# Tying each two-input GpSimd step to a VectorE step in a fused attention and gated-FFN kernel

## The chip, the cores and the metric

The kernel runs on one core of one Trainium2 chip. The metric is the device time of one execution in microseconds (us); lower is better. TensorE runs at one of two clock levels, 2.4 GHz (granted clock 1.00 in the profile) or 1.2 GHz (0.50).

## The reference

The reference first does attention over 8 batches, 8 heads, 576 positions and a head size of 64, with rotary position embedding on q and k, and then a gated feed-forward block:

```
q_rot, k_rot = rotate(q), rotate(k)                       # x1*cos - x2*sin, x1*sin + x2*cos
scores = matmul(q_rot, k_rot^T) / sqrt(64);  attn = softmax(scores)
x = matmul(attn, v)                                       # heads side by side: 576 x 512 a batch
gate_pre = sum over k = 0..4 of conv_w[k] * x shifted by k positions
out = (sigmoid(gate_pre) * (x @ w_val)) @ w_out
```

All of it is in fp32.

## The kernel before, in words

The work is cut into 32 pairs of heads (four pairs are one batch). All 32 pairs are unrolled. For a pair p the steps are:

- q and k are loaded with their halves also swapped, so that the rotation is two multiplications by a table (`rope_mul`, L275) and one addition (`rope_add`, L279). `qk_hi` (ScalarE) rounds the result to TensorE's fp32r type, and `qk_lo` (L303 for q, L306 for k) keeps the remainder; scores are made of three products of such parts.
- `s_mm` (TensorE, L331) makes scores of 128 rows by 576 in PSUM; there are two such score banks. `s_max` (VectorE, L337) reads them from PSUM and finds each row's maximum, `s_exp` (ScalarE, L345) reads them again and writes the exponentials to SBUF. A score bank is free for the next `s_mm` only after its `s_exp`.
- `t_mm` (TensorE) transposes the exponentials into PSUM, `t_copy` (ScalarE L430, VectorE L432) copies them to SBUF, `pv_mm` and `pv_left` (TensorE, L441 and L451) multiply by v. `r_inv` (VectorE, L461) inverts the sums, and `x_norm` (VectorE, L492, one input in PSUM) scales.
- `x_hi` (ScalarE) and `x_lo` (GpSimd, L505) split x as above. `tap` (VectorE, L518, taps 1 to 4) adds up the convolution, two SBUF inputs each, and `gate` (ScalarE) is its activation.
- After each fourth pair comes that batch's feed-forward part: `f_mm` (TensorE, L558) in two stages, `y_mul` (VectorE, L566, one input in PSUM), `y_hi` (ScalarE), `y_lo` (GpSimd, L573) and `o_out`.
- In the first quarter `weight_step` decodes the weights to such parts (L594 to L606, VectorE, ScalarE and GpSimd).

GpSimd's part is therefore 230 steps, each with two SBUF inputs: 63 `rope_mul`, 45 `rope_add`, 10 `qk_lo`, 15 `weight_step`, 33 `x_lo`, 64 `y_lo`.

What order do they run in? The jobs of all pairs are listed first with what each reads and writes. `ORDER`, a table of 3,327 entries, then says in which order they are issued; a letter after a number names the engine where there is a choice (V VectorE, A ScalarE, G GpSimd). Each engine works through its own entries in the order of the table. Between engines, only data holds a step back: a wait on a semaphore is made where a step reads or overwrites what another engine's step makes or uses. So GpSimd may run ahead of VectorE's place in the table, or fall behind it, as far as the data lets it. For instance, this is a piece of the table, where 1636 is `tap` 2 of pair 15 (VectorE), 1782V a `t_copy` and 1643 a `y_mul` on VectorE, and 1961G is one `rope_mul` of pair 19 on GpSimd:

```
1636 1966 1824:01 1782V 1643:0 1961G
```

Nothing ties 1961G to 1636; it waits for its input's DMA and for the buffers.

Of the kernel before, what the change touches and what calls it, by code (L numbers as in the profile page):

```python
# [10 lines left out]
F32 = mybir.dt.float32  # L11
# [3 lines left out]
AF = mybir.ActivationFunctionType  # L15
ALU = mybir.AluOpType
AX = mybir.AxisListType
# [8 lines left out]
G0 = 256  # L26
G1 = 320
SCALE = 0.125
W = 640
RAW = 1  # L30
# [134 lines left out]
"""  # L165
FILLS = {11: (32, 0), 17: (7, 1), 50: (19, 0), 63: (14, 2), 89: (7, 3), 101: (7, 0), 183: (2, 3), 287: (2, 1), 425: (2, 2)}


class Plan:

# [12 lines left out]

        self.jobs.append((engines, fn, args, r.split(), w.split()))

    def run(self, engine, fill):

        writer, sees = {}, []
        for i, (_, _, _, r, w) in enumerate(self.jobs):
            sees.append([writer.get(t) for t in r + w])  # L190
            writer.update(dict.fromkeys(w, i))
        writer = {}
        for step, entry in enumerate(ORDER.split()):
            entry, _, slots = entry.partition(":")
            i = int(entry.rstrip("VAG"))
            engines, fn, args, r, w = self.jobs[i]
            assert [writer.get(t) for t in r + w] == sees[i], entry
            writer.update(dict.fromkeys(w, i))
            if step in FILLS:
                fill(*FILLS[step])  # L200
            self.slots = [int(x) for x in slots]
            fn(*args, *([engine[entry[-1]]] if len(engines) > 1 else []))
            assert not self.slots, entry


@with_exitstack
def attn_gated_ffn(ctx: ExitStack, tc: tile.TileContext, q2, k2, v2, tab, w_val, conv_w, w_out, out, collect=None):
# [11 lines left out]
    NP = q2.shape[0]  # L219
    NB = out.shape[0]  # L220
    PPB = NP // NB
    V, A, G, T, SP = nc.vector, nc.scalar, nc.gpsimd, nc.tensor, nc.sync
# [7 lines left out]
    plan = Plan()  # L230
# [9 lines left out]
    table = const.tile([128, 2, W], F32, name="tab")  # L240
# [10 lines left out]
    xs = [const.tile([128, 4 + S], F32, name=f"x{i}") for i in range(2)]  # L251
    sums = [const.tile([128, 9], F32, name=f"sums{i}") for i in range(2)]

    state = {}
# [17 lines left out]

    def rope_mul(p, n, i, a, b, eng):
        t = ins[n]
        eng.tensor_tensor(out=t[:, i, a:b], in0=t[:, 0 if p < RAW else i, a:b], in1=table[:, i, a:b], op=ALU.mult)  # L275

    def rope_add(p, n, a, b, eng):
        t = ins[n][:, :, a:b]
        eng.tensor_tensor(out=t[:, 0], in0=t[:, 0], in1=t[:, 1], op=ALU.add)  # L279

    def rope_mm(p, n, a, b):

# [5 lines left out]
    def rotated(p, n, a, b):  # L288
        return state[p][f"b{n}{a}"][:, 0:b - a] if p < RAW else ins[n][:, 0, a:b]
# [9 lines left out]
    def qk_lo(p, n, a, b, eng=V):  # L299
        at = D if n == "k" else 0  # L300
        t = state[p][n][:, :, a + at:b + at]
        if n == "q":
            V.scalar_tensor_tensor(out=t[:, 1], in0=rotated(p, n, a, b), scalar=SCALE, in1=t[:, 0].bitcast(F32),  # L303
                                   op0=ALU.mult, op1=ALU.subtract)
        else:
            eng.tensor_tensor(out=t[:, 1], in0=rotated(p, n, a, b), in1=t[:, 0].bitcast(F32), op=ALU.subtract)  # L306

    def k_wrap(p):

# [24 lines left out]
    def s_max(p, i):  # L334
        st = state[p]
        st[f"nm{i}"] = ring("nm", [128, 1], F32, "nm")
        V.tensor_reduce(out=st[f"nm{i}"], in_=st[f"s{i}"], axis=AX.XY, op=ALU.max, negate=True)  # L337

    def s_exp(p, i, t, part):

# [60 lines left out]
    def t_copy(p, key, eng):  # L401
        both = key[:2] == "h1" and p < NP - 1
        bank = state[p]["bm" + key[2] if both else "b" + key]
        if key[0] == "m":
            x = "ab".index(key[1])
            src = bank[:, 0:256].rearrange("p (j x) -> p j x", x=D)
            dst = turned(p, 1)[:, x * 4:x * 4 + 4, 256:320]
        elif both:
            at = 128 + "ab".index(key[2]) * D
            src = bank[:, 256:384].rearrange("p (h x) -> p h x", h=2)  # L410
            dst = turned(p, "r")[:, :, at:at + D]
        elif key == "hm":
            src = bank[0:D, 0:128].rearrange("p (h x) -> p h x", h=2)
            dst = turned(p, "r")[0:D, :, 256:320]
        elif key[0] == "h" and p == NP - 1:
            rows = HEAD[1 - int(key[1])]
            src = bank[rows].rearrange("p (h x) -> p h x", h=2)
            dst = turned(p, "r")[rows, :, 0:256]
        elif key[0] == "h":
            at = int(key[1]) * 128  # L420
            src = bank[:, 0:256].rearrange("p (h x) -> p h x", h=2)
            dst = turned(p, "r")[:, :, at:at + 128]
        else:
            c = int(key[0])
            g = c // 2
            at = (c - 2 * g) * 128 + "ab".index(key[1]) * D
            src = bank.rearrange("p (s x) -> p s x", x=D)
            dst = turned(p, g)[:, :, at:at + D]
        if eng is A:
            A.copy(out=dst, in_=src)  # L430
        else:
            V.tensor_copy(out=dst, in_=src)  # L432

    def pv_mm(p, g, part):
        st = state[p]
# [22 lines left out]
    def r_inv(p, g):  # L458
        for a, b in COLS[g]:
            r = sums[p % 2][:, a:b]  # L460
            V.tensor_scalar(out=r, in0=r, scalar1=1e-9, scalar2=None, op0=ALU.add)  # L461
            V.reciprocal(out=r if p == NP - 1 else state[p]["pm"][:, 1, a:b], in_=r)

    def r_mm(p, g):
        bank = ring("ps_t", [128, 512], F32, "ps_r", psum)
# [23 lines left out]

    def x_norm(p, g):  # L490
        n = G1 if g else G0
        V.tensor_tensor(out=xs[p % 2][:, 4 + g * G0:4 + g * G0 + n], in0=state[p][f"a{g}"][:, 0:n],  # L492
                        in1=state[p]["rb"][:, g * G0:g * G0 + n], op=ALU.mult)

    def x_hi(p, a, b):
# [5 lines left out]
    def x_lo(p, a, b):  # L501
        st = state[p]
        if "xl" not in st:
            st["xl"] = ring("pl", [128, S], F32R, "xl")
        G.tensor_tensor(out=st["xl"][:, a:b], in0=xs[p % 2][:, 4 + a:4 + b], in1=st["xh"][:, a:b].bitcast(F32), op=ALU.subtract)  # L505

    def tap(p, k, a, b):
        st = state[p]
        c = p % PPB
        x_sb = xs[p % 2]  # L510
        w = cw[:, c * TAPS + k:c * TAPS + k + 1]
        if k == 0:
            if "g" not in st:
                st["g"] = ring("pg", [128, S], F32, "g")
            A.activation(out=st["g"][:, a:b], in_=x_sb[:, a:b], func=AF.Copy, scale=w)  # L515
        else:
            g = st["g"][:, a:b]
            V.scalar_tensor_tensor(out=g, in0=x_sb[:, a + k:b + k], scalar=w, in1=g, op0=ALU.mult, op1=ALU.add)  # L518

    def gate(p, a, b):  # L520

# [20 lines left out]
    ffn = {}  # L542
# [17 lines left out]
    def y_mul(b, dc, lo, hi):  # L560
        n = hi - lo
        if b not in ffn:
            ffn[b] = [ring(f"y{x}", [128, NCH, S], F32R, f"y{x}") for x in range(2)]
        y = ring("yy", [128, G1], F32, "y")[:, 0:n]
        ffn[b, "y", dc, lo] = y
        V.scalar_tensor_tensor(out=y, in0=state[b * PPB + dc]["g"][:, lo:hi], scalar=1.0, in1=ffn[b, 0, dc, lo][:, 0:n],  # L566
                               op0=ALU.add, op1=ALU.mult)

    def y_hi(b, dc, lo, hi):
        A.copy(out=ffn[b][0][:, dc, lo:hi], in_=ffn[b, "y", dc, lo])  # L570

    def y_lo(b, dc, lo, hi):
        G.tensor_tensor(out=ffn[b][1][:, dc, lo:hi], in0=ffn[b, "y", dc, lo], in1=ffn[b][0][:, dc, lo:hi].bitcast(F32),  # L573
                        op=ALU.subtract)

    def o_out(b, oc, lo, hi, eng):
        n = hi - lo
        o = ring("oo", [128, G1], F32, "o")[:, 0:n]
        if eng is A:
            A.activation(out=o, in_=ffn[b, 1, oc, lo][:, 0:n], func=AF.Copy, scale=0.5)  # L580
        else:
            V.tensor_scalar(out=o, in0=ffn[b, 1, oc, lo][:, 0:n], scalar1=0.5, scalar2=None, op0=ALU.mult)
        ffn[b, "o", oc, lo] = o

    def o_dma(b, oc, lo, hi):
        SP.dma_start(out=out[b, oc * 128:(oc + 1) * 128, lo:hi], in_=ffn[b, "o", oc, lo])
# [22 lines left out]
    taps = []  # L609
# [5 lines left out]
        taps.extend(decode(st, tmp, whole=cw))  # L615

    def tap_step(i):
        taps[i]()

    wsteps = {}  # L620

# [8 lines left out]
                              w_hi[n][:, c, m:m + x], w_lo[n][:, c, m:m + x])  # L630

    def weight_step(n, i, k, *eng):
        wsteps[n, i][k](*eng)

    def load_tab(a, b):
        A.dma_start(out=table[:, :, a:b], in_=tab[0, :, :, a:b])
# [40 lines left out]
    for p in range(NP):  # L677
# [7 lines left out]
        for n in ("k", "q"):  # L685
            cut = 288 if n == "k" else 384
            for a, b in [(0, wide[n])] if p else [(0, cut), (cut, wide[n])]:
                half = R2 if p else (1,) if a else (0,)
                x0, x1, hi, lo = (toks(f, half) for f in (f"{n}in#0.@", f"{n}in#1.@", f"{n}{par}#hi.@", f"{n}{par}#lo.@"))
                tr = toks("tab@", [i for i, (u, v) in enumerate(((0, 288), (288, S), (S, W))) if a < v and u < b])  # L690
                add("S", load, p, n, a, b, w=x0 if p < RAW else x0 + " " + x1)
                if p < RAW:
                    add("GV", rope_mul, p, n, 1, a, b, r=tr + " " + x0, w=x1)
                    add("GV", rope_mul, p, n, 0, a, b, r=tr, w=x0)
                    for i, (x, y) in enumerate(((0, cut), (cut, wide[n]))):
                        if not a <= x < b:
                            continue
                        bank, hi, lo = f"ps_t/{n}{p}.{i}", f"{n}{par}#hi.{i}", f"{n}{par}#lo.{i}"
# [13 lines left out]
        for i, c in enumerate(order(p) + (4,)):  # L712
            r = kr + f" k{par}#w" * (i % 2) + " " + toks(f"q{par}#@.@", ("hi", "lo"), (0,) if c < 3 else R2)
            add("P", s_mm, p, c, i % 2, r=r, w=toks(f"ps_s/{p}.@", (2 * c, 2 * c + 1)[:1 + (c < 4)]))
            for x in (2 * c, 2 * c + 1)[:1 + (c < 4)]:
                t = f"{i // 2}{x % 2}" if c < 4 else "m"
# [5 lines left out]
        for key in [str(c) for c in order(p)] + ["m", "h0"] + ["h1"] * last + ["hm"]:  # L722
            g = "r" if key[0] == "h" else 1 if key in ("m", "2", "3") else 0
            if key in ("m", "hm"):
                r = f"p/{p}.m#8" + f" p/{p}.m#r" * (key == "hm" and not last)
                if key == "m" and not last:
                    r += " " + " ".join(f"p/{p}.1{h}#{2 * c + h}" for c in order(p)[2:4] for h in R2)
            elif key[0] == "h":
                i = int(key[1])
                r = " ".join(f"p/{p}.{i}{h}#{2 * c + h}" for c in order(p)[2 * i:2 * i + 2] for h in R2)  # L730
# [72 lines left out]
                    add("S", o_dma, b, *a, r=f"oo/{b}.{j}")  # L803
    if collect is not None:
        return plan
    with tc.manual_schedule():
        plan.run({"V": V, "A": A, "G": G}, fill)


# [57 lines left out]
```

## Time and profile before

| | |
|---|---|
| median of 3 runs | 695.62 us (695.5 to 698.72) |
| the profiled execution | 699.4 us, with a span of 697.5 us on the core |
| busy share of the span | TensorE 96%, VectorE 84%, ScalarE 72%, GpSimd 44% |

The profile is one execution, with each instruction's start and duration. An engine's busy share is an average over the whole span, so the stages have to be looked at apart. The chain of work that ended last is followed back from the last instruction: at each step to what released it, or to the instruction in front on its own engine. Matmuls are pipelined, and their ends are modelled.

### The profile page before, as it was taken

Reading aid. Unit: us, or ns where it says so; the run is one execution under the profiler, and the core shown is the slowest. Engines: PE = TensorE matmul, PEld = TensorE weight load, DVE = VectorE, ACT = ScalarE, POOL = GpSimd, SP = SyncE. Lnnn points to the kernel's source line nnn. Section 1 sums busy time; section 2 is a strip of 40 time slices with the busy share of each in tenths; the row PEclk is TensorE's granted clock in tenths of the full one; section 3 lists DMA queues with packets and bytes.
Section 4 is the critical chain, followed back from the end, with each engine's and each line's share of the span. In section 5 each row is a group of like instructions: output and inputs, shape, how many; then the busy total and the mean of one; then the engine's idle time right before and its main releaser. Section 6 shows DMA issues by size and latency. Waiting matters only on the chain.

```text
span 697.5 us, 18207 instructions
## 1 busy us (share of the span) xinstructions
PE 669.6 (96%) x7184; PEld 539.9 (77%) x7184; DVE 585.9 (84%) x1012; ACT 504.4 (72%) x1238; POOL 308.1 (44%) x236
## 2 busy tenths in 40 slices
PE   8888899899999999999999999999999999999998
PEld 7656567677778888787878888777788887788887
DVE  5998899999988868989899887998889889787741
ACT  3787877786877887778669877677678786777522
POOL 1344424264354765456334554366445553243031
PEclk9997769999999999999999999999999999999999
DMA  6344332433443143243432152433422144411011
GB/s 222 109 135 142 102 112 75 117 105 103 140 140 105 60 136 121 60 125 112 132 105 82 58 167 78 133 103 114 131 97 65 61 128 123 132 47 35 27 61 68
DMA packets 47318, 72.65 MB, mean 104 GB/s; under 512 B 15961, under 2 KB 25730, under 8 KB 47234
## 3 DMA queue, kind: packets, MB, share of 16 engines
q1 hardware_dynamic: 46690, 70.91, 32.8%
q8 instruction: 56, 0.92, 0.6%
q10 hardware_dynamic: 544, 0.59, 0.3%
q14 instruction: 28, 0.23, 0.1%
HBM read 61.89 MB, written 9.59 MB: 102 GB/s over the span
## 4 chain that ended last, share of the span: by engine, by line
PE 79%; DVE 12%; ACT 6%; issue 3%; POOL 0%; DVEq 0%; ACTq 0%; POOLq 0%
PE ps_f L558 27%; PE ps_s L331 18%; PE ps_a L441 17%; PE ps_t L392 10%; DVE nm L337 4%; ACT p L345 3%; PE ps_a L451 3%; PE ps_t L357 2%; DVE g L518 2%; ACT pt L430 2%; PE ps_t L352 1%; DVE q L303 1%; DVE pt L432 1%; PE ps_r L286 1%; ACT q L295 0%
## 5 line engine op out<-in xcount | busy, mean ns | idle before, releaser
L345 ACT ACTIVATE p<-ps_s,nm 128x576 f32<-128x576 f32 x288 | 212.7, 742 | 70.7 <-DVE nm L337 68.5
L337 DVE TENSOR_REDUCE nm<-ps_s 128x1 f32<-128x576 f32 x288 | 207.9, 750 | 44.7 <-PE ps_s L331 40.4
L331 PE MATMUL ps_s<-k,q 64*128 64x288 f32 (+1 forms) x1728 | 184.4, 315 | 14.6 <-ACT p L345 14.0
L331 PEld LDWEIGHTS ps_s<-k,q 64*128 64x128 f32 (+1 forms) x1728 | 143.6, 190 | 48.0 <-ACT p L345 33.7
L430 ACT COPY pt<-ps_t 128x512 f32<-128x512 f32 (+1 forms) x228 | 120.9, 547 | 54.8 <-PE ps_t L392 52.9
L441 PE MATMUL ps_a<-pt,v 128*64 128x256 f32 (+1 forms) x1024 | 139.9, 416 | 1.2 <-DVE pr L432 0.7
L518 DVE SCALAR_TENSOR_TENSOR g<-x,cw,g 128x576 f32<-128x576 f32 (+1 forms) x132 | 121.0, 918 | 1.4 <-ACT g L515 0.9
L392 PEld LDWEIGHTS ps_t<-ident,p 64*128 64x128 f32 x2428 | 101.5, 141 | 22.4 <-issue 9.6
L392 PE MATMUL ps_t<-ident,p 64*128 64x64 f32 x2428 | 113.4, 229 | 3.9 <-ACT p L345 1.3
L558 PE MATMUL ps_f<-y,wout_hi 128*128 128x288 f32 (+2 forms) x512 | 107.4, 302 | 0.7 <-DVE pt L432 0.5
L441 PEld LDWEIGHTS ps_a<-pt,v 128*64 128x64 f32 x1024 | 68.8, 138 | 46.9 <-issue 3.8
L573 POOL TENSOR_TENSOR y<-y,y 128x288 fp32r<-128x288 f32 (+2 forms) x64 | 57.2, 905 | 105.0 <-ACT y L570 101.6
L558 PEld LDWEIGHTS ps_f<-y,wout_hi 128*128 128x128 f32 x512 | 81.4, 188 | 6.4 <-issue 1.5
L275 POOL TENSOR_TENSOR qin<-qin,tab 128x640 f32<-128x640 f32 (+1 forms) x36 | 58.2, 1627 | 55.1 <-DMA qin<-in_q 44.0
L558 PE MATMUL ps_f<-xh,wval_hi 128*128 128x288 f32 (+2 forms) x256 | 79.1, 313 | 1.1 <-ACT pt L430 1.1
L558 PE MATMUL ps_f<-xh,wval_lo 128*128 128x288 f32 (+2 forms) x256 | 76.4, 301 | 0.0
L558 PE MATMUL ps_f<-xl,wval_hi 128*128 128x288 f32 (+2 forms) x256 | 75.5, 298 | 0.0
L558 PE MATMUL ps_f<-y,wout_lo 128*128 128x288 f32 (+2 forms) x256 | 74.4, 294 | 0.0
L275 POOL TENSOR_TENSOR kin<-kin,tab 128x576 f32<-128x576 f32 x27 | 43.7, 1625 | 62.7 <-DMA kin<-in_k 52.1
L505 POOL TENSOR_TENSOR xl<-x,xh 128x576 fp32r<-128x576 f32 (+2 forms) x33 | 48.2, 1463 | 50.6 <-ACT xh L499 31.1
L432 DVE COPY pt<-ps_t 128x512 f32<-128x512 f32 (+1 forms) x92 | 56.8, 623 | 5.3 <-PE ps_t L392 4.7
L345 ACT ACTIVATION_READ_ACCUMULATOR p<-ps_s,nm 128x1 f32 x288 | 57.3, 199 | 0.0
(87 smaller groups left out, 860.9 us busy)
## 6 DMA issues: line engine op xcount, KB each, us to landing
kin<-in_k SPq DMA_DIRECT2D x31, 576.0 KB
qin<-in_q SPq DMA_DIRECT2D x31, 512.0 KB
v<-in_v SPq DMA_DIRECT2D x32, 320.0 KB
out_t<-o SPq DMA_DIRECT2D x56, 144.0 KB
rb<-rd SPq DMA_DIRECT2D x31, 144.0 KB
rb<-rd SPq DMA_DIRECT2D x31, 128.0 KB
wst<-in_w_val SPq DMA_DIRECT2D x4, 512.0 KB
wst<-in_w_out SPq DMA_DIRECT2D x8, 256.0 KB
```

The lines of the kernel that those rows point to most:

```text
L275: eng.tensor_tensor(out=t[:, i, a:b], in0=t[:, 0 if p < RAW else i, a:b], in1=table[:, i, a:b], op=ALU.mult)
L331: T.matmul(out=tiles[h][:, half, 0:288], lhsT=st["q"][rows, x, c * 128:c * 128 + 128], rhs=st["k"][rows, y, k0:k0 + 288], start=(i == 0), ...
L337: V.tensor_reduce(out=st[f"nm{i}"], in_=st[f"s{i}"], axis=AX.XY, op=ALU.max, negate=True)
L345: A.activation(out=st[f"p{t}"][:, part].rearrange("p (b x) -> p b x", b=2), in_=st[f"s{i}"], func=AF.Exp, bias=st[f"nm{i}"], scale=1.0, ac ...
L392: T.transpose(out=st["b" + key + x][:, k * D:(k + 1) * D], in_=src[rows], identity=ident[rows, rows])
L430: A.copy(out=dst, in_=src)
L432: V.tensor_copy(out=dst, in_=src)
L441: T.matmul(out=st[f"a{g}"][HEAD[h], 0:n], lhsT=st["v"][:, j, h, :], rhs=st[f"pt{g}"][:, h * 4 + j], start=(j == 0), stop=False)
L505: G.tensor_tensor(out=st["xl"][:, a:b], in0=xs[p % 2][:, 4 + a:4 + b], in1=st["xh"][:, a:b].bitcast(F32), op=ALU.subtract)
L518: V.scalar_tensor_tensor(out=g, in0=x_sb[:, a + k:b + k], scalar=w, in1=g, op0=ALU.mult, op1=ALU.add)
L558: T.matmul(out=acc[:, 0:n], lhsT=wt[w][:, kc, ds], rhs=mv, start=(kc == 0 and i == 0), stop=(kc == NCH - 1 and i == 2))
L573: G.tensor_tensor(out=ffn[b][1][:, dc, lo:hi], in0=ffn[b, "y", dc, lo], in1=ffn[b][0][:, dc, lo:hi].bitcast(F32), op=ALU.subtract)
```

## The change: what it does

While the table is issued, the program remembers VectorE's latest instruction and, whenever VectorE gets a step of the kinds in `PORT`, the instruction that stood in front of that step. Each GpSimd step then gets one dependency more: on that remembered instruction. In the piece of the table above, 1961G now waits until VectorE has finished what it runs in front of 1636 (a `qk_lo` of q). It doesn't wait for 1636 itself. The functions return their instruction so that this can be done; no step changes its engine, its order, its operands or its buffers. `x_norm`, `y_mul` and `r_inv` are not in `PORT`.

```
+PORT = {"rope_mul", "rope_add", "qk_lo", "tap", "weight_step"}
...
-    def run(self, engine, fill):
-
+    def run(self, engine, fill, behind):
+        before = latest = None
...
-            fn(*args, *([engine[entry[-1]]] if len(engines) > 1 else []))
+            on = entry[-1] if len(engines) > 1 else engines
+            inst = fn(*args, *([engine[on]] if len(engines) > 1 else []))
             assert not self.slots, entry
+            if on == "V":
+                if fn.__name__ in PORT:
+                    before = latest
+                latest = inst.ins
+            elif on == "G" and inst is not None and before is not None:
+                behind(inst.ins, before)
...
+    def behind(inst, other):
+        tc.add_manual_dep(inst, other.name, mybir.DependencyInfo(mybir.DependencyClass.Sync, mybir.DependencyReason.DATA), reason="order")
+
     with tc.manual_schedule():
-        plan.run({"V": V, "A": A, "G": G}, fill)
+        plan.run({"V": V, "A": A, "G": G}, fill, behind)
```

## Rows read from the trace of the kernel before

**Rows 1.** The page: the span, and each engine's busy time, its share and its number of instructions.

```profile
span 697.5 us, 18207 instructions
PE 669.6 (96%) x7184; PEld 539.9 (77%) x7184; DVE 585.9 (84%) x1012; ACT 504.4 (72%) x1238; POOL 308.1 (44%) x236
```

**Rows 2.** The windows: four stretches (their bounds and length in us), then each engine's busy us and number of instructions, the granted clock of TensorE, and the DMAs.

```profile
60.40:74.00 13.60, 11.98 (x88) 9.18 (x90) 11.44 (x23) 10.66 (x28) 5.61 (x4) 0.50 0.34 102
74.00:84.30 10.30, 8.76 (x106) 5.69 (x104) 8.45 (x15) 7.77 (x19) 3.97 (x3) 1.00 0.46 157
84.30:97.90 13.60, 11.65 (x102) 9.02 (x98) 12.48 (x22) 10.94 (x28) 4.99 (x4) 0.50 0.21 66
149.00:660.00 511.00, 504.38 (x5656) 410.11 (x5656) 440.36 (x729) 388.38 (x952) 246.11 (x180) 1.00 0.33 100
```

**Rows 3.** The durations of lines L518, L303, L279, L606 and L337: shortest, median and longest in ns, first and last start in us, and shapes. The last row is of the view by line and shape: busy us and the mean ns of one.

```profile
L518 DVE SCALAR_TENSOR_TENSOR g<-x,cw,g x132: 476/811/2134, 45.8 to 675.8; 128x576 f32<-128x576 f32 x124, 128x256 f32<-128x256 f32 x4, 128x320 f32<-128x320 f32 x4
L303 DVE SCALAR_TENSOR_TENSOR q<-qin,q x31: 802/817/2030, 30.2 to 623.4; 128x640 fp32r<-128x640 f32 x31
L279 DVE TENSOR_TENSOR qin<-qin x10: 815/820/1960, 28.1 to 569.9; 128x640 f32<-128x640 f32 x10
L279 POOL TENSOR_TENSOR kin<-kin x24: 1399/1424/2002, 22.7 to 615.4; 128x576 f32<-128x576 f32 x24
L606 DVE TENSOR_TENSOR wout_lo<-wst x3: 365/426/1184, 128.6 to 150.8; 128x256 fp32r<-128x256 f32 x3
L337 DVE TENSOR_REDUCE nm<-ps_s x288: 696/749/760, 14.4 to 654.4; 128x1 f32<-128x576 f32 x144
L518 DVE SCALAR_TENSOR_TENSOR g<-x,cw,g 128x576 f32<-128x576 f32 x124 | 116.6, 941 | 1.2 <-ACT g L515 0.6
```

**Rows 4.** The timeline from 357 to 361.5 us, three of its lines: start and duration in us, and in brackets the engine's idle time before it and what ended it.

```profile
358.00 1.41 POOL L275 TENSOR_TENSOR kin<-kin,tab 128x576 f32<-128x576 f32 x1 [6.49 <-DMA kin<-in_k]
358.04 1.99 DVE L518 SCALAR_TENSOR_TENSOR g<-x,cw,g 128x576 f32<-128x576 f32 x1
...
360.28 1.07 PE L392 MATMUL ps_t<-ident,p 64*128 64x64 f32 x16 [0.62 <-DVE pr L432]
```

**Rows 5.** The timeline from 104 to 107 us, two of its lines.

```profile
104.42 0.82 DVE L275 TENSOR_TENSOR qin<-qin,tab 128x640 f32<-128x640 f32 x1
104.58 1.92 POOL L279 TENSOR_TENSOR kin<-kin 128x576 f32<-128x576 f32 x1 [1.66 <-DVE kin L275]
```

**Rows 6.** The timeline of GpSimd and of VectorE at the first and at the last of 37 places, and at one between them (a line with x2 is two instructions in a row).

```profile
8.13 0.90 POOL L275 TENSOR_TENSOR qin<-qin,tab 128x256 f32<-128x256 f32 x1 [6.83 <-DMA wst<-in_w_val]
8.36 1.68 DVE L275 TENSOR_TENSOR qin<-qin,tab 128x384 f32<-128x384 f32 x2
...
418.46 1.41 POOL L275 TENSOR_TENSOR kin<-kin,tab 128x576 f32<-128x576 f32 x1 [7.92 <-DVE q L303]
...
419.77 0.75 DVE L275 TENSOR_TENSOR kin<-kin,tab 128x576 f32<-128x576 f32 x1
...
421.70 0.75 DVE L279 TENSOR_TENSOR kin<-kin 128x576 f32<-128x576 f32 x1
...
584.58 2.85 DVE L518 SCALAR_TENSOR_TENSOR g<-x,cw,g 128x576 f32<-128x576 f32 x2
...
585.07 1.74 POOL L275 TENSOR_TENSOR qin<-qin,tab 128x640 f32<-128x640 f32 x1 [3.89 <-DMA qin<-in_q]
```

**Rows 7.** The chain that ended last: its shares by engine, and nine of its pieces (start and duration in us; "issue" is time in which the engine waited for nothing that the profile shows).

```profile
PE 79%; DVE 12%; ACT 6%; issue 3%; POOL 0%; DVEq 0%; ACTq 0%; POOLq 0%
...
150.77 1.18 DVE wout_lo L606
155.38 1.20 DVE qin L279
279.27 1.86 DVE g L518
350.32 1.58 DVE qin L279
358.12 1.90 DVE g L518
468.08 1.95 DVE g L518
498.26 1.69 issue
499.96 2.02 DVE q L303
519.47 1.89 DVE g L518
```

**Rows 8.** The waits of TensorE from 149 to 660 us: what waited for what, us in total, times, and the longest.

```profile
PE ps_s L331 <- ACT p L345: 3.1, 6, 1.2
PE ps_t L392 <- ACT pt L430: 0.7, 1, 0.7
PE ps_a L441 <- DVE pr L432: 0.7, 1, 0.7
PE ps_t L392 <- DVE pr L432: 0.6, 1, 0.6
PE ps_f L558 <- DVE pt L432: 0.5, 1, 0.5
PE ps_f L558 <- DVE pr L432: 0.2, 1, 0.2
```

More of the change, by code (lines that the diff above doesn't have):

```diff
@@ L274, in rope_mul @@
         t = ins[n]
-        eng.tensor_tensor(out=t[:, i, a:b], in0=t[:, 0 if p < RAW else i, a:b], in1=table[:, i, a:b], op=ALU.mult)
+        return eng.tensor_tensor(out=t[:, i, a:b], in0=t[:, 0 if p < RAW else i, a:b], in1=table[:, i, a:b], op=ALU.mult)
     def rope_add(p, n, a, b, eng):
         t = ins[n][:, :, a:b]
-        eng.tensor_tensor(out=t[:, 0], in0=t[:, 0], in1=t[:, 1], op=ALU.add)
+        return eng.tensor_tensor(out=t[:, 0], in0=t[:, 0], in1=t[:, 1], op=ALU.add)
     def rope_mm(p, n, a, b):
@@ L302, in qk_lo @@
         if n == "q":
-            V.scalar_tensor_tensor(out=t[:, 1], in0=rotated(p, n, a, b), scalar=SCALE, in1=t[:, 0].bitcast(F32),
-                                   op0=ALU.mult, op1=ALU.subtract)
+            return V.scalar_tensor_tensor(out=t[:, 1], in0=rotated(p, n, a, b), scalar=SCALE, in1=t[:, 0].bitcast(F32),
+                                          op0=ALU.mult, op1=ALU.subtract)
         else:
-            eng.tensor_tensor(out=t[:, 1], in0=rotated(p, n, a, b), in1=t[:, 0].bitcast(F32), op=ALU.subtract)
+            return eng.tensor_tensor(out=t[:, 1], in0=rotated(p, n, a, b), in1=t[:, 0].bitcast(F32), op=ALU.subtract)
     def k_wrap(p):
@@ L336, in s_max @@
         st[f"nm{i}"] = ring("nm", [128, 1], F32, "nm")
-        V.tensor_reduce(out=st[f"nm{i}"], in_=st[f"s{i}"], axis=AX.XY, op=ALU.max, negate=True)
+        return V.tensor_reduce(out=st[f"nm{i}"], in_=st[f"s{i}"], axis=AX.XY, op=ALU.max, negate=True)
     def s_exp(p, i, t, part):
@@ L429, in t_copy @@
         if eng is A:
-            A.copy(out=dst, in_=src)
-        else:
-            V.tensor_copy(out=dst, in_=src)
+            return A.copy(out=dst, in_=src)
+        return V.tensor_copy(out=dst, in_=src)
     def pv_mm(p, g, part):
@@ L461, in r_inv @@
             V.tensor_scalar(out=r, in0=r, scalar1=1e-9, scalar2=None, op0=ALU.add)
-            V.reciprocal(out=r if p == NP - 1 else state[p]["pm"][:, 1, a:b], in_=r)
+            inst = V.reciprocal(out=r if p == NP - 1 else state[p]["pm"][:, 1, a:b], in_=r)
+        return inst
     def r_mm(p, g):
@@ L491, in x_norm @@
         n = G1 if g else G0
-        V.tensor_tensor(out=xs[p % 2][:, 4 + g * G0:4 + g * G0 + n], in0=state[p][f"a{g}"][:, 0:n],
+        return V.tensor_tensor(out=xs[p % 2][:, 4 + g * G0:4 + g * G0 + n], in0=state[p][f"a{g}"][:, 0:n],
                         in1=state[p]["rb"][:, g * G0:g * G0 + n], op=ALU.mult)
@@ L504, in x_lo @@
             st["xl"] = ring("pl", [128, S], F32R, "xl")
-        G.tensor_tensor(out=st["xl"][:, a:b], in0=xs[p % 2][:, 4 + a:4 + b], in1=st["xh"][:, a:b].bitcast(F32), op=ALU.subtract)
+        return G.tensor_tensor(out=st["xl"][:, a:b], in0=xs[p % 2][:, 4 + a:4 + b], in1=st["xh"][:, a:b].bitcast(F32), op=ALU.subtract)
     def tap(p, k, a, b):
@@ L517, in tap @@
             g = st["g"][:, a:b]
-            V.scalar_tensor_tensor(out=g, in0=x_sb[:, a + k:b + k], scalar=w, in1=g, op0=ALU.mult, op1=ALU.add)
+            return V.scalar_tensor_tensor(out=g, in0=x_sb[:, a + k:b + k], scalar=w, in1=g, op0=ALU.mult, op1=ALU.add)
     def gate(p, a, b):
@@ L565, in y_mul @@
         ffn[b, "y", dc, lo] = y
-        V.scalar_tensor_tensor(out=y, in0=state[b * PPB + dc]["g"][:, lo:hi], scalar=1.0, in1=ffn[b, 0, dc, lo][:, 0:n],
+        return V.scalar_tensor_tensor(out=y, in0=state[b * PPB + dc]["g"][:, lo:hi], scalar=1.0, in1=ffn[b, 0, dc, lo][:, 0:n],
                                op0=ALU.add, op1=ALU.mult)
@@ L572, in y_lo @@
     def y_lo(b, dc, lo, hi):
-        G.tensor_tensor(out=ffn[b][1][:, dc, lo:hi], in0=ffn[b, "y", dc, lo], in1=ffn[b][0][:, dc, lo:hi].bitcast(F32),
-                        op=ALU.subtract)
+        return G.tensor_tensor(out=ffn[b][1][:, dc, lo:hi], in0=ffn[b, "y", dc, lo], in1=ffn[b][0][:, dc, lo:hi].bitcast(F32),
+                               op=ALU.subtract)
     def o_out(b, oc, lo, hi, eng):
@@ L579, in o_out @@
         if eng is A:
-            A.activation(out=o, in_=ffn[b, 1, oc, lo][:, 0:n], func=AF.Copy, scale=0.5)
+            inst = A.activation(out=o, in_=ffn[b, 1, oc, lo][:, 0:n], func=AF.Copy, scale=0.5)
         else:
-            V.tensor_scalar(out=o, in0=ffn[b, 1, oc, lo][:, 0:n], scalar1=0.5, scalar2=None, op0=ALU.mult)
+            inst = V.tensor_scalar(out=o, in0=ffn[b, 1, oc, lo][:, 0:n], scalar1=0.5, scalar2=None, op0=ALU.mult)
         ffn[b, "o", oc, lo] = o
+        return inst
     def o_dma(b, oc, lo, hi):
@@ L617, in tap_step @@
     def tap_step(i):
-        taps[i]()
+        return taps[i]()
     wsteps = {}
@@ L632, in weight_step @@
     def weight_step(n, i, k, *eng):
-        wsteps[n, i][k](*eng)
+        return wsteps[n, i][k](*eng)
     def load_tab(a, b):
```

## The prediction

> **What bounds the kernel now.** I began with the busy shares: TensorE 96%, VectorE 84%, GpSimd 44% [rows 1]. GpSimd, the engine whose steps get the new wait, is far from being the bound. An average hides stages, so the windows came next [rows 2]. From 149 to 660 us TensorE is busy 504.4 of 511 us at the granted clock 1.00 (2.4 GHz): there it sets the pace, and about 6.6 us of visible idle time can be won. In the first 98 us it is less busy, and in two long stretches its clock is 0.50 (1.2 GHz).
>
> Then I read how long VectorE's two-input steps take, because a delay that isn't a wait doesn't show in a list of waits. A `tap` takes 811 ns in the median and 2,134 ns at most; the `q` remainder 817 and 2,030; the `rope_add` of q 820 and 1,960 [rows 3]. The reader should set beside them `s_max`, as big, but with its input in PSUM: 749 in the median and never over 760. So something stretches just the steps that read two inputs from SBUF. The timeline shows what: GpSimd starts a `rope_mul` at 358.00, VectorE starts its tap 0.04 us later, and the tap takes 1.99 us in place of 0.81 [rows 4]. GpSimd's step ends at 359.41, and the tap's end, 360.03, is about 0.62 after that. The opposite order is there too: VectorE starts at 104.42 and takes an undisturbed 0.82; GpSimd starts at 104.58 and takes 1.92 where 1.42 is usual [rows 5, 3]. Whoever starts first runs at full speed, and the other pays.
>
> How much is lost? The taps of 576 columns alone have a mean of 941 against the median 811: 0.13 x 124 = 16.1 us [rows 3]. Over all VectorE steps I count 48 that are stretched, by 31 us together.
>
> How much of that matters? The chain of work that ended last is 79% TensorE and 12% VectorE, and nine of its pieces are, or sit behind, such stretched steps [rows 7].
>
> **The change part by part.** *What it removes.* I went down the table with the trace: for each of the 230 GpSimd steps I took the VectorE step that the new wait names, and compared its end with the GpSimd step's start. In 193 cases it has ended before; the wait costs nothing there, and nothing moves. In 37 cases the GpSimd step starts earlier and will be held, by 28.2 us together: the first is that of 8.13 us, the last that of 585.07 [rows 6]. Of the 48 stretched VectorE steps 28 are stretched by one of these 37, and they hold 23.0 of the 31 us (the first of them is at 8.36, the last is the second tap of the line at 584.58 [rows 6]). For them the order of starting turns round: VectorE's instructions overlap by some 0.1 us, so the two-input step is under way when its predecessor's end lets GpSimd go. Rows 5 show just this pattern in the kernel before: that GpSimd step was released by the `kin` step in front of the one at 104.42. So about 23 of VectorE's 586 us should go.
>
> *What of it is on the path.* From above: the nine pieces of the chain, each less its undisturbed duration [rows 7, 3]. 150.77: 1.18 - 0.43 = 0.75. 155.38: 0.38. 279.27: 1.86 - 0.81 = 1.05. 350.32: 0.76. 358.12: 1.09. 468.08: 1.14. 498.26 (the next step stands behind a tap that was stretched): 1.69 - 0.68 = 1.01. 499.96: 2.02 - 0.82 = 1.20. 519.47: 1.08. Sum 8.5 us. That is too much if another path is close behind. From the other side: TensorE's idle time from 149 to 660 us is 3.1 + 0.7 + 0.7 + 0.6 + 0.5 + 0.2 = 5.8 us [rows 8], and apart from one gap of 0.2 us it lies within 6 us behind one of the stretched steps; 360.28 is one such gap [rows 4]. That is too little, since a matmul's modelled end reaches past the start of the next, so that short stalls don't show. I take the middle, 7.1 us. The other 16 us of VectorE's gain hide behind TensorE.
>
> *What it adds.* A held GpSimd step now runs behind its VectorE step and ends 1.2 us later on average (from 0.1 to 3.4). What is queued behind it is GpSimd's next step; in 193 of 230 cases nothing changes, and the engine has 56% of its time free. Who waits for the held step itself? In most places another GpSimd step or an `f_mm`, more than 1.3 us later; where it is GpSimd's next step, the two move together. The tightest place is at 418.46: that `rope_mul` will start behind VectorE's step of 419.77 and end at about 421.9 instead of 419.87, while VectorE's `rope_add` that needs it starts at 421.70 [rows 6]. Price 0.2 us, once; nothing if VectorE is late, and up to 1.4 us if GpSimd is late by a whole step more. The loads of the next q and k stand behind this chain on SP's queue; they move by as much, and on no row does TensorE wait for a load [rows 8].
>
> The held step now occupies the shared path behind the VectorE step, so VectorE's next steps are the ones to look at. In 28 of 37 places these are `s_max`, copies from PSUM, `x_norm` or `y_mul` for as long as GpSimd's step lasts, none of which is stretched by it [rows 3]. In nine places a two-input step comes too soon, by 1.6 us together. The chain carries 8.5 of 23, so I count 0.37 x 1.6 = 0.6 us.
>
> The waits themselves: the trace has no row for a wait that is already met. From below nothing; from above the 0.16 us between the two starts of rows 5 for each of the 37 steps that really wait, 5.9 us of GpSimd's time, hidden in its free 56%. I take zero on the path; with that cover gone it would be 0.37 x 5.9 = 2.2 us.
>
> *The first 149 us.* No piece of the chain there is a moved one [rows 7], though two steps on VectorE (8.36 and 94.40) get shorter by 0.5 and 1.2 us. I count 0.4 for the first, as everything follows it, and none for the second, where TensorE runs at 0.50.
>
> *Sum:* -7.1 + 0.2 + 0.6 - 0.4 = -6.7 us. The profiled execution's own 699.4 us become 692.7. It was 3.8 us above the median of the runs; against the 695.62 of that median the same difference gives 688.9, say 689.
>
> *A rule of the notes against the trace.* The Trainium skill, "SBUF — State Buffer", sections "SBUF: two separate sides" and "Who interferes with whom", says that VectorE and GpSimd share one port pair, that a VectorE step with two SBUF inputs contends with a GpSimd step that reads SBUF, and that the order of issue decides which of them blocks, fully. Rows 4 and 5 agree on who pays. On the size they don't quite: blocked fully, the tap would have ended 0.81 us behind GpSimd's 359.41, and it took 0.62; at the full price the chain's nine pieces would be worth some 1.7 us more.
>
> **The rivals.** *The gain is hidden.* TensorE is 98.7% busy in the long middle [rows 2]; if the copies or ScalarE's exponentials end just behind VectorE's steps, less than half of 7.1 comes through: 3 us, 692.5. Against it: the gaps of rows 8 sit right behind stretched steps.
>
> *GpSimd wins the race.* The held step is let go just as VectorE's two-input step starts. If GpSimd took the path first, all 37 places would stretch VectorE by about 1.2 us, 44 us in place of 23. At 0.37 that is 8 us more: 703.5, slower. It decides when GpSimd's start comes before VectorE's; the margin is the 0.16 us of rows 5, there in VectorE's favour.
>
> By the page named above it would be just this order of issue that decides; the trace agrees in rows 4 and 5.
>
> *TensorE's clock moves.* In 13.6 us at 0.50 it did 88 and 102 matmuls, against 106 in 10.3 us at 1.00 [rows 2], though the mix differs: 3.7 to 5.1 us lost in each stretch. TensorE is idle there for 1.6 to 2.0 us even at the slow clock, so small shifts can mend or widen what lies in front of such a stretch. One stretch less gives 684.5, one more 693.5.
>
> *It does nothing.* If the named steps had always ended first, the time would stay at 695.6. Against it: 37 starts that are earlier.
>
> **How the numbers follow.** The measurement can tell about 0.5% (3.5 us) from no change. My forecast, between 5 and 10 us less: 0.66. A stretch of slow clock less on top: 0.08. Hidden to within 3.5 us: 0.10. A slow stretch more: 0.05. Nothing: 0.03. GpSimd first, or another wait at the tight places: 0.08. So faster 0.74, same 0.18, slower 0.08. The likeliest is 689. The range starts at 683, below the 684.5 of the rival with the better clock by the 1.5 us between my middle value and the chain's sum. It ends at 695, which takes in the hidden gain, the extra slow stretch and the 2.2 us of uncovered waits. The forecast's own range is 686 to 691.
>
> **What would show it.** In the profile after: the maximum of the taps (2,134) falls, and their mean of 941 comes near 840; VectorE's busy time falls from 586 to about 565; GpSimd's busy time grows, since its steps are now the stretched ones; TensorE's idle time between 149 and 660 us falls from 5.8 to under 2; the chain has less than 12% of VectorE. I would be wrong if taps are stretched as often as before (GpSimd first, or collisions one step later), if GpSimd's waits for VectorE end on the chain, or if the granted clock changes.

## The result, and the profile after

| | before | after |
|---|---|---|
| median of 4 runs | 696.43 us (695.5 to 698.72) | 686.01 us (683.66 to 688.54) |
| the profiled execution | 699.4 us, span 697.5 | 686.14 us, span 684.3 |

The ratio is 0.9846, with an interval from 0.9802 to 0.9890. The change makes the kernel faster by 1.5%, 10.4 us of the medians; 6.7 us were forecast. The time lies inside the range (683 to 695) and, by a hair, inside the forecast's own range (686 to 691), at its fast end; the gain lies just beyond the 5 to 10 us that were given the largest chance.

The page after: the span, the engines' busy time, and the chain's shares by engine. They answer to [rows 1] and to the first of [rows 7].

```profile
span 684.3 us, 18228 instructions
PE 660.7 (97%) x7184; PEld 534.7 (78%) x7184; DVE 563.5 (82%) x1012; ACT 504.3 (74%) x1238; POOL 311.6 (46%) x236
...
PE 82%; DVE 8%; ACT 5%; DMA 2%; issue 2%; SPq 1%; POOL 0%; ACTq 0%; DVEq 0%; POOLq 0%
```

VectorE does the same 1,012 instructions in 22.4 us less, GpSimd its 236 in 3.5 us more, and VectorE's share of the chain falls from 12% to 8%.

The durations of the taps after (L518 is L531 now; shortest, median and longest in ns), and their row by line and shape (busy us, mean ns). They answer to [rows 3].

```profile
L531 DVE SCALAR_TENSOR_TENSOR g<-x,cw,g x132: 476/810/1394, 45.0 to 662.7; 128x576 f32<-128x576 f32 x124, 128x256 f32<-128x256 f32 x4, 128x320 f32<-128x320 f32 x4
L531 DVE SCALAR_TENSOR_TENSOR g<-x,cw,g 128x576 f32<-128x576 f32 x124 | 102.5, 827 | 1.2 <-ACT g L528 0.6
```

The median stays, the longest falls from 2,134 to 1,394 and the mean from 941 to 827. Over all of VectorE I count 25 stretched steps with 7.4 us, where it was 48 with 31.0. One of the 25 still lies behind one of the 37 held steps: a `rope_mul` at 316.16 us, 0.60 us longer for a `y_lo` that starts 0.58 us ahead of it. The wait names the step in front of the `rope_mul` before that one, so it can't help here.

How that looks, in the timeline: the same tap and the same `rope_mul` as in [rows 4].

```profile
351.63 0.81 DVE L531 SCALAR_TENSOR_TENSOR g<-x,cw,g 128x576 f32<-128x576 f32 x1
...
351.85 1.88 POOL L288 TENSOR_TENSOR kin<-kin,tab 128x576 f32<-128x576 f32 x1 [5.21 <-DVE q L316]
```

Before, GpSimd started 0.04 us ahead of the tap and the tap took 1.99. Now GpSimd waits for the `qk_lo` in front of the tap (q L316), starts 0.22 us behind the tap, and it is GpSimd's step that takes 1.88 in place of 1.41.

The waits of TensorE after, from 149 to 650 us (what waited for what, us in total, times, longest). They answer to [rows 8].

```profile
PE ps_f L571 <- DVE pt L444: 1.3, 1, 1.3
PE ps_f L571 <- DVE pr L444: 0.2, 1, 0.2
PE ps_s L344 <- ACT p L358: 0.2, 1, 0.2
```

1.7 us are left of 5.8, and 1.3 of them have another cause, a late load of q. The chain after shows it (start and duration in us):

```profile
330.30 0.58 SPq L280
...
332.53 4.92 DMA qin<-in_q
...
337.58 0.82 DVE qin L288
338.40 0.61 DVE pt L444
...
339.06 1.33 PE ps_f L571 x8
```

SP issues the three loads from 330.30 on, and the last of them lands 7.2 us behind the first issue; before, the same load was issued at 337.61 and its `rope_mul` on VectorE started at 342.10, 4.5 us later. VectorE stands still for 4.5 us, and the lead that the `s_max` steps have on those of before falls here from 7.3 to 4.9 us before it grows again. In the profile of the first experiment below the same load makes no such gap. I take it for the accident of one execution.

The granted clock, in the windows after (bounds and length, busy us and instructions of TensorE, its weight loads, VectorE, ScalarE and GpSimd, then the clock). They answer to [rows 2].

```profile
60.40:74.00 13.60, 12.52 (x114) 9.52 (x116) 11.44 (x22) 11.21 (x32) 6.37 (x5) 0.77 0.34 106
74.00:84.30 10.30, 6.84 (x95) 4.70 (x91) 10.30 (x18) 9.03 (x20) 5.17 (x4) 0.97 0.48 154
84.30:97.90 13.60, 13.12 (x108) 9.39 (x110) 11.39 (x25) 10.81 (x29) 3.40 (x3) 0.64 0.39 117
149.00:650.00 501.00, 499.00 (x5618) 407.53 (x5617) 419.16 (x726) 385.55 (x944) 245.50 (x177) 1.00 0.33 102
```

This execution had 17 us at 0.50, that of before 31 us. So the two profiled executions, 13.3 us apart, do not measure the change; the medians do. Whether the clock has a share in these is a question for the experiments.

### The profile page after: what moved, and what is told of

It reads as the page before. It is cut to its first block, busy times and chain, and to the rows that moved or that the text cites. A ratio compares the mean times of both kernels' runs of the same rounds, so it can differ in the third digit from the quotient of the medians.

```text
span 684.3 us, 18228 instructions
## 1 busy us (share of the span) xinstructions
PE 660.7 (97%) x7184; PEld 534.7 (78%) x7184; DVE 563.5 (82%) x1012; ACT 504.3 (74%) x1238; POOL 311.6 (46%) x236
## 4 chain that ended last, share of the span: by engine, by line
PE 82%; DVE 8%; ACT 5%; DMA 2%; issue 2%; SPq 1%; POOL 0%; ACTq 0%; DVEq 0%; POOLq 0%
PE ps_f L571 29%; PE ps_s L344 19%; PE ps_a L453 16%; PE ps_t L405 10%; DVE nm L350 3%; PE ps_a L463 3%; PE ps_t L370 3%; ACT p L358 2%; DMA qin<-in_q 1%; ACT pt L443 1%; PE ps_t L365 1%; DVE g L531 1%; PE ps_r L299 1%; DVE qin L288 1%; DVE kin L288 1%
## 5 line engine op out<-in xcount | busy, mean ns | idle before, releaser
L344 PE MATMUL ps_s<-k,q 64*128 64x288 f32 (+1 forms) x1728 | 180.3, 313 | 11.7 <-ACT p L358 11.5
L344 PEld LDWEIGHTS ps_s<-k,q 64*128 64x128 f32 (+1 forms) x1728 | 141.4, 189 | 43.1 <-ACT p L358 28.7
L405 PEld LDWEIGHTS ps_t<-ident,p 64*128 64x128 f32 x2428 | 100.0, 140 | 20.5 <-issue 9.0
L405 PE MATMUL ps_t<-ident,p 64*128 64x64 f32 x2428 | 111.5, 227 | 2.5 <-ACT p L358 1.3
L531 DVE SCALAR_TENSOR_TENSOR g<-x,cw,g 128x576 f32<-128x576 f32 (+1 forms) x132 | 106.9, 812 | 1.4 <-ACT g L528 0.9
L586 POOL TENSOR_TENSOR y<-y,y 128x288 fp32r<-128x288 f32 (+2 forms) x64 | 58.6, 926 | 100.1 <-ACT y L583 89.7
L288 POOL TENSOR_TENSOR kin<-kin,tab 128x576 f32<-128x576 f32 x27 | 46.3, 1718 | 70.2 <-DVE g L531 12.7
L518 POOL TENSOR_TENSOR xl<-x,xh 128x576 fp32r<-128x576 f32 (+2 forms) x33 | 48.9, 1485 | 50.5 <-ACT xh L512 26.9
L444 DVE COPY pt<-ps_t 128x512 f32<-128x512 f32 (+1 forms) x92 | 56.8, 623 | 6.0 <-PE ps_t L405 5.5
```

What stands on the lines that cost most here:

```text
L288: return eng.tensor_tensor(out=t[:, i, a:b], in0=t[:, 0 if p < RAW else i, a:b], in1=table[:, i, a:b], op=ALU.mult)
L344: T.matmul(out=tiles[h][:, half, 0:288], lhsT=st["q"][rows, x, c * 128:c * 128 + 128], rhs=st["k"][rows, y, k0:k0 + 288], start=(i == 0), ...
L405: T.transpose(out=st["b" + key + x][:, k * D:(k + 1) * D], in_=src[rows], identity=ident[rows, rows])
L444: return V.tensor_copy(out=dst, in_=src)
L518: return G.tensor_tensor(out=st["xl"][:, a:b], in0=xs[p % 2][:, 4 + a:4 + b], in1=st["xh"][:, a:b].bitcast(F32), op=ALU.subtract)
L531: return V.scalar_tensor_tensor(out=g, in0=x_sb[:, a + k:b + k], scalar=w, in1=g, op0=ALU.mult, op1=ALU.add)
```

## The experiments

Theory: the gain is the order of starting at the 37 places where a GpSimd step is really held. Rivals: the other 193 waits matter too; TensorE's clock has moved; and, for the size, either the chain names all places that matter or it has left some out. Times are medians; a ratio is to the kernel before on the same chip.

**Only the 37 waits.** The numbers are places in the table.

```
+HELD = {20, 55, 357, 411, 652, 682, 688, 700, 711, 948, 1343, 1391, 1398, 1448, 1543, 1558, 1674, 1691, 1734,
+        1754, 1789, 1886, 2041, 2161, 2279, 2289, 2435, 2442, 2477, 2483, 2525, 2534, 2545, 2628, 2732, 2827, 2847}
...
-            elif on == "G" and inst is not None and before is not None:
+            elif on == "G" and inst is not None and before is not None and step in HELD:
```

> The new wait is given only to the 37 GpSimd steps that start before the named VectorE step's end in the trace of the kernel before. Theory (only the order of starting at the shared path matters): all of the gain, 684 to 689 us, VectorE busy about 564 us, and the taps' mean near 812 ns. Rival (the wait paces GpSimd as a whole, and the 193 waits that were met at once in the old trace hold as soon as the rest moves): less than the whole gain, 690 us or more, because other GpSimd steps come to lie in front of two-input VectorE steps.

685.58 us (684.47 to 686.51), ratio 0.9841 [0.9819, 0.9864]. From its page, and its TensorE waits from 149 to 650 us:

```profile
PE 662.0 (97%) x7184; PEld 535.7 (78%) x7184; DVE 564.2 (83%) x1012; ACT 504.3 (74%) x1238; POOL 311.4 (46%) x236
```

```profile
PE ps_f L572 <- DVE pr L445: 0.2, 1, 0.2
PE ps_s L345 <- ACT p L359: 0.2, 1, 0.2
```

All the gain is here, and without the late load TensorE's idle time in the long middle is 0.4 us. The taps' mean is 830, not the 812 expected.

**Only the other 193.** The same list, with `step not in HELD`.

> The wait is given only to the other 193 GpSimd steps. Theory: no change, 694 to 698 us, VectorE busy about 586 us, taps' mean near 920 ns. Rival (pacing): a part of the gain, 692 us or less.

695.95 us (694.9 to 700.76), ratio 0.9988 [0.9967, 1.0009]: no change. The page:

```profile
PE 666.7 (96%) x7184; PEld 537.0 (77%) x7184; DVE 579.5 (84%) x1012; ACT 504.9 (73%) x1238; POOL 307.9 (44%) x236
```

VectorE was to stay at 586 and fell to 579.5, with 44 stretched steps and 24.8 us. That isn't the work of these waits: the GpSimd steps that start close behind the step named are the same here as in the kernel before, and the kernel before with the fills (below), which has none of these waits, shows 581.0. The stretch differs by some us from execution to execution, and the 6.2 us less of it here didn't reach the end. 193 waits that are met cost nothing that can be measured.

**The wait one VectorE step further ahead.** GpSimd is let go a step too early.

```
-        before = latest = None
+        before = latest = older = None
...
-                    before = latest
-                latest = inst.ins
+                    before = older
+                older, latest = latest, inst.ins
```

> All 230 steps wait, but for the VectorE step one further ahead, so that GpSimd is let go some 0.75 us before the two-input step starts and takes the shared path first. Theory (whoever starts first runs, the other pays): VectorE's two-input steps are stretched by about 0.6 us in about 37 places, 20 us together, VectorE busy 580 us or more, time 692 to 698 us. Rival (any hold on GpSimd helps, the place doesn't matter): as the changed kernel, 686 us.

699.65 us (697.43 to 701.94), ratio 1.0049 [1.0028, 1.0069]: slower than before, by about 3 us, and beyond the 692 to 698 us expected. It has as many waits as the change, and 51 stretched steps with 30.2 us, about what the kernel before has; VectorE is busy for 584.4 us. The chain's shares, and one place in the timeline:

```profile
PE 74%; DVE 15%; ACT 6%; issue 3%; DMA 0%; SPq 0%; POOL 0%; DVEq 0%; ACTq 0%; POOLq 0%
```

```profile
579.74 1.41 POOL L288 TENSOR_TENSOR kin<-kin,tab 128x576 f32<-128x576 f32 x1 [4.41 <-DVE pt L444]
579.78 1.99 DVE L531 SCALAR_TENSOR_TENSOR g<-x,cw,g 128x576 f32<-128x576 f32 x1
```

A copy (pt L444), one step further ahead, lets GpSimd go; it starts 0.04 us before the tap, and the tap takes 1.99 us. At 21 places GpSimd starts within 0.26 us of the end of the step named, and 19 stretched VectorE steps with 16.1 us lie beside them. This is the rival "GpSimd wins the race". What pays is therefore which of the two starts first, and not that GpSimd runs later. Why the kernel is 3 us slower than before, with no more stretch, isn't shown.

The rule can be counted. In the traces of all twelve kernels a GpSimd step starts during 499 two-input VectorE steps that no other GpSimd step disturbs at their start. In 498 the VectorE step keeps its usual time to within 0.07 us. The one exception stands in this trace: a tap at 496.96 takes 2.08 us, and GpSimd's step starts only 0.04 us behind it. Other leads that small were enough, so there the order can't be read off the profile.

**The wait on the two-input step itself.** GpSimd starts when VectorE's step is over.

```
             if on == "V":
+                latest = inst.ins
                 if fn.__name__ in PORT:
                     before = latest
-                latest = inst.ins
```

> All 230 steps wait for the two-input VectorE step itself, not for the one in front of it. Theory: VectorE is as undisturbed as in the changed kernel (busy about 563 us), GpSimd is no longer stretched by that step (busy about 295 us in place of 312), its results come some 0.1 us later, and the time is 685 to 688 us, no different from the changed kernel. Rival (GpSimd's later start costs on the path): 689 us or more.

687.65 us (686.49 to 690.14), ratio 0.9881 [0.9848, 0.9914]. The page, and the place of [rows 4] once more:

```profile
PE 662.6 (97%) x7184; PEld 536.7 (78%) x7184; DVE 570.6 (83%) x1012; ACT 504.3 (74%) x1238; POOL 285.5 (42%) x236
```

```profile
352.24 0.81 DVE L531 SCALAR_TENSOR_TENSOR g<-x,cw,g 128x576 f32<-128x576 f32 x1
...
353.18 1.42 POOL L288 TENSOR_TENSOR kin<-kin,tab 128x576 f32<-128x576 f32 x1 [5.64 <-DVE g L531]
```

Both steps are undisturbed, and GpSimd is busy for 26 us less than with the change. But VectorE has 570.6 us and not the 563 expected: 54 steps are stretched, by 15.3 us together. Of these, 26 with 5.4 us lie beside a GpSimd step that starts within 0.26 us of the end of the step it waits for, and so runs into one of VectorE's next steps. The ratio's interval overlaps that of the change; that it is a little worse isn't shown.

**TensorE's clock.** Four fills more, 34 dummy transposes of TensorE in four places between 44 and 87 us, to shorten the two stretches that ran at 0.50, in the kernel before and in the one after. They change no result. The profiled executions have 7 and 14 us at 0.50, in place of 31 and 17.

```
+FILLS.update({176: (5, 3), 191: (8, 2), 350: (9, 1), 364: (12, 2)})
```

> The kernel before, with 34 more dummy transposes on TensorE in four places between 44 and 87 us where it waits for ScalarE. If the time at the slow clock is what makes runs of one kernel differ (0.978 of full clock: 699.8 us; 0.990: 693.9 us), and the transposes shorten it to under 10 us: 690 to 694 us. If they only delay TensorE: 697 us or more.

> The changed kernel with the same 34 transposes. If the change's gain has nothing to do with the clock: about 10.5 us less than the kernel before with the transposes (679 to 684 us). If a part of its gain came from a better clock: the two come nearer to each other, 8 us or less apart.

Before with the fills: 693.39 us (691.13 to 695.21), ratio 0.9967 [0.9946, 0.9987]. After with the fills: 684.52 us (683.68 to 685.68), ratio 0.9835 [0.9808, 0.9862]. Both now have a mean clock of 0.990 to 0.995 in every run, and they are still 8.9 us apart. So most of the gain, 8.9 of 10.4, is there at an equal clock; whether the last 1.5 us were luck with the clock the intervals don't tell. The traces show the gain where the clock has no part in it: from 147 to 652 us, all at 1.00, the lead of the `s_max` steps over those of before grows by 10.1 us with the 37 waits alone, from 3.6 to 13.8. That the clock alone is worth something can be seen in 17 runs of before (those beside the last experiment): the ones with a mean clock of 0.977 to 0.980 took 697.7 to 699.4 us, the ones with 0.987 to 0.988 took 693.1 to 696.6. Changed and filled, this is the fastest of all the kernels by its median, 1.5 us below the change alone, but the two ratios' intervals overlap.

**Moving the stretched steps away.** On top of the change, 15 GpSimd entries of the table are moved right behind the VectorE step that they still stretched (here one: 2521G and 2522V are the two `rope_mul` of k of pair 24), without the fills and with them.

```
-2298:1 2521G 2264 2318A:0
...
-2265:3 2522V 2301
+2298:1 2264 2318A:0
...
+2265:3 2522V 2521G 2301
```

> The changed kernel, with 15 of the GpSimd steps that still stretch a VectorE step (25 such places, 7.4 us) put in the table right behind that VectorE step, so that they wait for the step in front of it too. Theory: the stretching falls to under 3 us, VectorE busy 559 us, and at 0.6 us of time for each us of VectorE the time falls by 2 to 3 us, 683 to 684 us. Rival (these GpSimd results are needed at once): 686 us or more, with a wait for GpSimd on the chain.

> Both of the last two together: the moves and the transposes add up, 677 to 682 us, if each does what its theory says; otherwise as the better one of the two alone.

687.79 us (687.02 to 690.31), ratio 0.9892 [0.9863, 0.9921], and with the fills 685.51 us (684.71 to 686.75), ratio 0.9855 [0.9831, 0.9879]: no gain in either pair, where 683 to 684 and 677 to 682 were expected. Without the fills 22 steps are still stretched, by 10.8 us, and new waits appear. VectorE waits once for GpSimd, 1.3 us for a `rope_mul` of k that takes 2.59 us and stands on the chain at 215.51, as the rival had it; and these are TensorE's waits from 149 to 650 us:

```profile
PE ps_t L274 <- DVE pt L313: 1.3, 1, 1.3
PE ps_s L213 <- ACT p L227: 0.8, 2, 0.7
```

So the moves leave more stretch than there was (10.8 us in place of 7.4), and waits besides. What the 7.4 us that the change leaves are worth at the end stays open.

**Where the size went wrong: nine steps, or 28.** Of the 37 waits, first only the nine whose GpSimd steps stretch what stands in the nine chain pieces of [rows 7], then only the other 28.

```
+HELD = {688, 711, 1343, 1691, 1734, 2279, 2435, 2442, 2525}
```

> The new wait for nine GpSimd steps only: those that stretch the VectorE steps in, or in front of, the nine pieces of the chain of the kernel before. They hold 9.3 of the 23.0 us of stretch (0.82 + 0.38 + 1.13 + 1.14 + 1.18 + 1.23 + 1.09 + 1.21 + 1.16). VectorE should be busy for about 577 us. Theory 1 (the chain names the places, and the nine pieces were only priced too low): all the gain is here, 8.5 to 10.4 us less than the kernel before. Theory 2 (the chain left places out, and what reaches the end goes by the stretch taken away, about 10.4 / 23.0 = 0.45 of it): 4.2 us less.

> The new wait for the other 28 of the 37 held GpSimd steps. They hold 13.7 us of stretch, none of it in the nine pieces of the chain. VectorE should be busy for about 572 us. Theory 1 (the chain names the places): within 1 us of the kernel before; the prediction counted 0.4 us for the step of 8.36 us and nothing for the rest. Theory 2 (the chain left places out): 0.45 x 13.7 = 6.2 us less. If both kernels gain, and their gains add up to more than 10.4 us, several paths run side by side and one of them alone can be relieved only until the next one sets the end.

The nine: 689.45 us (687.47 to 691.74), ratio 0.9895 [0.9867, 0.9923], 7.2 us less. The 28: 692.73 us (689.56 to 694.62), ratio 0.9945 [0.9924, 0.9966], 3.9 us less. Together 11.1, as much as all 37 gave beside their own runs of before (11.2). Neither theory holds. Chain places do weigh more: the gain is 7.2 for 9.3 us of stretch, against 3.9 for 13.7. But the others aren't free. The long middle of each, in the windows:

```profile
149.00:650.00 501.00, 499.25 (x5622) 406.82 (x5619) 425.22 (x720) 387.31 (x949) 248.40 (x179) 1.00 0.34 102
```

```profile
149.00:650.00 501.00, 496.61 (x5588) 403.92 (x5587) 422.73 (x719) 384.00 (x942) 245.01 (x177) 1.00 0.33 102
```

The first is that of the nine, the second that of the 28. TensorE starts 5,622 and 5,588 matmuls in these 501 us. The kernel before started 5,549:

```profile
149.00:650.00 501.00, 494.38 (x5549) 401.87 (x5548) 431.96 (x711) 382.50 (x938) 246.11 (x180) 1.00 0.33 101
```

The 28 have no single place. Against before, the same `s_max` steps come 4.9 us earlier at 158 us (clock included) and 8.5 us earlier at 602; what lies between is all at clock 1.00. The lead grows near 201 us (by 0.4), from 356 to 370 (by 1.1) and near 585 (by 1.4), and by less than 0.3 elsewhere; 0.9 us won near 320 are lost again by 325. From 147 to 652 us it grows by 3.2 us for the 28, by 6.9 for the nine and by 0.9 for the 193 of above.

The split isn't clean, since a place can be relieved by a small move of the two engines too. In the trace of the nine, the stretch at 585 us is gone though its wait isn't there, and 0.95 of the 6.9 us are won there; that of the 193 wins 1.2 there in the same way. In the trace of the 28, the tap of 358.04, one of the nine places, is not stretched, and 0.8 of the 3.2 us are won there. And of the nine places not all gave what their pieces say: in the trace of the nine 468.08 gave 1.2 us, 498.26 and 499.96 together 1.9, and 519.47 nothing.

The place near 585 us was on the chain of the kernel before, and I had read past it. That chain around 585 us:

```profile
584.66 0.74 DVE g L518
585.40 0.03 issue
585.43 0.79 DVE g L518
586.22 0.11 issue
...
586.44 0.47 issue
...
586.96 0.39 issue
587.35 0.69 DVE pt L432
588.04 0.04 issue
588.08 1.87 PE ps_f L558 x12
```

The stretched second tap stands there with an ordinary 0.79 us. Its stretch is in the pieces called "issue" behind it, up to 587.35: there VectorE was still busy with the tap. And the 0.5 us for which `ps_f` waits for `pt` in [rows 8] is the gap that follows. With the 28 waits the two taps and the copy behind them read, in the timeline:

```profile
576.82 1.67 DVE L532 SCALAR_TENSOR_TENSOR g<-x,cw,g 128x576 f32<-128x576 f32 x2
...
578.40 0.68 DVE L445 COPY pt<-ps_t 128x512 f32<-128x512 f32 x1
```

1.67 where [rows 6] have 2.85. The `s_max` steps stand 7.1 us ahead of those of before at 577, 7.8 at 582 and 8.5 at 602: the first growth goes with another of the 28, a tap of 580.33 that is stretched before and not here, the second with this place.

## Why the prediction was right, and where its size was off

- **The mechanism: right.** Who starts first runs undisturbed; the wait turns the order round at the 37 places (in the profiles of the 193 and of before with the fills, 31 and 33 of these steps start early: the list is that of one execution). The 37 alone give all of the gain, the 193 none, and a wait one step too early makes the kernel slower than before.
- **VectorE's gain: right.** From 586 to about 565 was forecast; it is 563.5. A recount of the trace before puts 26 of the stretched steps, not 28, beside the 37, with the same 23.0 us; and as the stretch differs from execution to execution (the 193 waits and the fills alone show 579.5 and 581.0), the agreement to 1.5 us is partly luck. The taps' mean was to come near 840 and is 827. GpSimd's busy time grows, by 3.5 us. TensorE's idle time in the middle was to fall below 2 and is 1.7 with the late load.
- **The nine pieces: right.** Taken at 7.1 us, between 5.8 and 8.5; alone they gave 7.2 (the interval of the ratio makes that 5.4 to 9.3). That the two agree to 0.1 us is luck: 7.1 is the middle of two bounds, and about one of the 7.2 us was won at a place outside the nine.
- **"The other 16 us of VectorE's gain hide behind TensorE": wrong.** This term was mis-sized. The steps outside the nine gave 3.9 us more. I had two bounds and believed that both covered all places. The chain's sum left out what it shows as "issue" at 585 us. And a chain is one path: as I read it, a delay that it passes by on TensorE still counts where VectorE is only a little ahead; no run isolates that at a single place. TensorE's idle time was known to be too low, since a modelled end hides short stalls; I used it for one end of the middle value all the same.
- **New collisions, +0.6, and the tight place at 418.46, +0.2: too dear, as far as the profile shows.** After the change 7.4 us of stretch are left, not the 8.0 of before that the 37 don't cause, plus 1.6; four new collisions hold 1.0 of them. The profile after lists no wait of VectorE for GpSimd; that `rope_mul` starts at 412.63, takes 1.80, and the `rope_add` starts right behind it at 414.46, 0.04 us after the copy in front of it on VectorE has ended.
- **The first 149 us, -0.4:** not separated. The clock differs there from execution to execution, and no experiment isolates it.
- **The rivals.** "Hidden" and "does nothing" fall with the result. "GpSimd wins the race" didn't happen, but it is close by: a wait that names one VectorE step earlier brings it about at 21 places. "The clock moves": it does from run to run, of either kernel; at an equal clock 8.9 us of the gain remain.
- **The page of the Trainium skill.** On who pays ("SBUF — State Buffer", section "Who interferes with whom") the rows shown here agree, most plainly the pair of 579.74 and 579.78; the tap of 496.96, which lost with a lead of 0.04 us, is the one case that doesn't. Its full block, at which the nine pieces would be worth 1.7 us more, isn't needed: they gave 7.2.

## What to carry to other kernels

Compare the longest duration of an instruction with its median before reading any list of waits: here the shared path showed only there, and in the chain some of it hid under "issue". If VectorE is near the bound and GpSimd isn't, let GpSimd's step wait for the VectorE step *in front of* the one that it would stretch; one step earlier does harm, and a step later was no better. When sizing the gain, price the places on the chain at most of their stretch and the rest not at nothing. Here the medians give 0.78 and 0.28, and the traces at clock 1.00, with the places that were relieved by accident left out, about 0.64 (5.9 of 9.3) and 0.18 (2.4 of 13.7); that is one kernel.

## What the runs showed of the hardware

A small step with one input is held too. `r_inv` begins with an addition on 128x9 elements in SBUF, 167 ns in the median and up to 693 before the change. Three lines of the timeline after:

```profile
523.11 0.44 DVE L579 SCALAR_TENSOR_TENSOR y<-g,ps_f 128x288 f32<-128x288 f32 x1
523.16 1.42 POOL L319 TENSOR_TENSOR k<-kin,k 128x576 fp32r<-128x576 f32 x1 [0.87 <-ACT k L310]
...
524.12 0.49 DVE L473 TENSOR_SCALAR sums<-sums 128x9 f32<-128x9 f32 x1 [0.57 <-ACT p L358]
```

`y_mul`, with one input in PSUM, and GpSimd's `qk_lo` overlap and both take their usual time. The small addition starts in the middle of `qk_lo` and ends at 524.61, 0.03 us behind it. So "two inputs from SBUF" is too narrow a description of what GpSimd stretches on VectorE. `PORT` leaves this step out, and it is among the 25 that are still stretched.

The Trainium skill, "SBUF — State Buffer", section "Who interferes with whom", does name `tensor_scalar` among the operations that can take the shared ports when their operands meet certain conditions. That this one was held agrees with it; that it ran in the mode meant there, no row shows. I had looked only for steps with two inputs.
